# Causal attention with a channel mix: the reciprocals of the softmax sums go through TensorE as two fp16 parts instead of one fp32 operand, under a new plan

## The chip, the cores and the metric

The kernel runs on one core of one Trainium2 chip. The metric is the device time of one execution in microseconds, as the median of several runs. Three runs of the kernel before gave 539.42, 539.99 and 540.07 us.

## The reference

The inputs are `q`, `k`, `v` of shape (4, 12, 448, 64): 4 batches, 12 heads, 448 positions, head size 64, all fp32. Causal attention is followed by a channel mix with weights of 768 x 1024, 1024 x 768 and 768 x 768:

```python
scores = scale * np.matmul(q, k.transpose(0, 1, 3, 2))
scores = np.where(mask, -1000000000.0, scores)
scores = scores - np.max(scores, axis=-1, keepdims=True)
attn = np.exp(scores)
attn = attn / (np.sum(attn, axis=-1, keepdims=True) + 1e-09)
x = np.matmul(attn, v)          # heads side by side: (4, 448, 768)
x_prev = x moved down by one position
xk = mu_k * x + (1.0 - mu_k) * x_prev
xr = mu_r * x + (1.0 - mu_r) * x_prev
k = np.maximum(xk @ w_k, 0.0)
out = sigmoid(xr @ w_r) * (k * k @ w_v)
```

## The kernel before

The work is cut into 24 windows `w`, one for each pair of heads (6 pairs in each of 4 batches), and for each batch three rows of matmuls of the channel mix: `mk` (w_k), `mr` (w_r) and `mv` (w_v), all recorded at line 975.

A window goes through these steps. `score` (line 595) makes the scores of two heads, in fp32, as rows of 112 queries (4 chunks of 112), and adds the mask with small bf16 matmuls (line 616). `row_max` (line 630) takes the maxima on VectorE. `exps` (line 641) makes the exponentials on ScalarE, scaled up by 2^14, and adds up their sums into a tile `su` of 112 x 4 x 2: for each row of a chunk, 4 chunks and 2 heads. The exponentials stay undivided: `prob_hi` and `prob_lo` split them into two fp16 parts (lines 681 to 686), a transposing DMA turns them (line 692), and `weighted` (line 727) multiplies them with the values, 36 matmuls for a window (line 748); the first six windows are turned by TensorE in fp32 instead (`turn_e`, line 699), and take 24 matmuls at line 748.

The division is made at the end, on the transposed result, in which one position is one column. So the reciprocal of each sum has to stand in all 64 partitions of its head. That is done by four steps: `least` (line 658, ScalarE) adds the small constant to the sums, `recip` (line 661, VectorE) takes the reciprocals in place, `spread` (line 664, TensorE) multiplies a column of reciprocals, read as 64 equal columns, with the identity, so that row p of the chunk becomes column p in 64 partitions, and `spread_out` (line 678, VectorE or ScalarE) copies the result from PSUM to `xt`. `evac` (line 763) then multiplies the attention's result with `xt` and with a scale `xe` (line 938).

`spread` issues 8 fp32 matmuls for a window, 4 chunks by 2 heads. The two heads write to the lower and to the upper 64 partitions of one PSUM tile, from two column halves of TensorE. The profile shows each fp32 matmul as two records, 16 for a window. The tile has the tag `t`, whose pool has one buffer (line 386); the small steps that find one maximum over all partitions (`across`, line 448) and the idle matmuls share it.

The order of all instructions on all engines is made by a planner when the kernel is built (class `Plan`, line 35). Each step is entered by `plan.op` with its engine or engines, a cost in ns and the tiles that it reads and writes; steps that may run on one of several engines take ScalarE, VectorE or GpSimd as the plan has it, unless `by` in `CHOICE` (line 329) pins one. `l_load`, `l_att`, `l_wgh`, `l_mix`, `l_w` and `l_moe` in `CHOICE` lift a window's steps in the order, and `likes` favours engines. Every engine then works through its list in that order and waits, in order, for what an instruction needs. The planner fills long gaps of TensorE in the first 130 us with matmuls on a constant (`idle`, line 477). The four steps are entered in `weigh` (lines 1188 to 1199).

Of the kernel before, what the change touches and what calls it, by code (L numbers as in the profile page):

```python
# [11 lines left out]
F16 = mybir.dt.float16  # L12
# [3 lines left out]
AF = mybir.ActivationFunctionType  # L16
# [6 lines left out]
UP = 2.0**14  # L23
# [11 lines left out]
class Plan:  # L35
# [294 lines left out]
    "l_load": [-153, 304, 385, 144, 28, 153, 97, 60, -8, 105, 71, -20, 26, -303, 104, 894, -269, -9, -112, 27, 360, 271, -333, -282],  # L330
    "l_att": [-426, 60, 399, 122, 744, 836, 98, 213, 442, 308, 537, -143, -65, -254, 23, -108, -392, 2, 265, -623, 293, -35, -394, -101],
    "l_wgh": [201, -192, 134, 105, 94, 212, -70, -131, -5, 139, 268, 116, -88, 295, 32, -86, -103, -156, 1120, -19, 1254, 938, 84, 835],
    "l_mix": [4, 292, 190, 660, -23, -11, 615, -473, 183, 448, 126, -46, 601, 94, 297, 280, 72, 199, -539, -476, -538, -604, -1325, -922],
    "l_w": [568, 667, 632, -153, 139, 803, 1412, -163, 24, 385, 393, 544, 359, -208],
    "l_moe": [-11, -221, -117, 160, 236, -171, -183, -96, -366, 86, -327, -989],
    "chain": ["S", "S", "S", "S"],
    "ring": ["m", "m", "s", "s", "m", "m"],
    "pv": ["F", "F", "F", "F", "F", "F", "H", "H", "H", "H", "H", "H", "H", "H", "H", "H", "H", "H", "H", "H", "H", "H", "H", "H"],
    "likes": {"k_hi.DVE": 130, "w_lo.POOL": 0, "w_hi.ACT": -10750, "max_v.ACT": -70, "w_z.POOL": -100, "mix_lo.POOL": 270, "max_v.DVE": 430, "prob_hi.POOL": 800, "mix.DVE": 30, "r_copy.DVE": 30, "w_hi.DVE": -400, "parts_v.ACT": 30, "diff.POOL": 0, "w_hi.POOL": -1100, "mix.POOL": 0, "relu.DVE": 30, "prob_hi.ACT": 0, "r_copy.ACT": 180, "w_z.ACT": 0, "w_lo.DVE": 0, "whole.ACT": -1400, "w_z.DVE": 0, "mix_hi.ACT": -220, "relu.ACT": -1830, "k_hi.POOL": -160, "whole.DVE": 930, "diff.DVE": -100, "copy_e.DVE": 3060, "mix_hi.DVE": 210, "parts_v.POOL": 6050, "parts_v.DVE": 0, "mix_hi.POOL": 1170, "k_lo.POOL": -1000, "k_lo.DVE": -2100, "square.DVE": 370, "k_hi.ACT": -520, "mix_lo.DVE": 1300, "copy_e.ACT": -1000, "prob_lo.DVE": 1560, "prob_lo.POOL": -300, "spread_out.ACT": 1670, "spread_out.DVE": 570, "square.ACT": 0, "prob_hi.DVE": 1010},
# [6 lines left out]
def tile_causal_attention_channel_mix(  # L346
# [30 lines left out]

    const = ctx.enter_context(tc.tile_pool(name="const", bufs=1))
    wts = ctx.enter_context(tc.tile_pool(name="wts", bufs=1))
    act = ctx.enter_context(tc.tile_pool(name="act", bufs=1))  # L380
    p1 = ctx.enter_context(tc.tile_pool(name="p1", bufs=1))
    p2 = ctx.enter_context(tc.tile_pool(name="p2", bufs=2))
    ps_s = ctx.enter_context(tc.tile_pool(name="ps_s", bufs=NS, space=PSUM))
    ps_x = ctx.enter_context(tc.tile_pool(name="ps_x", bufs=1, space=PSUM))
    ps_m = ctx.enter_context(tc.tile_pool(name="ps_m", bufs=2, space=PSUM))
    ps_t = ctx.enter_context(tc.tile_pool(name="ps_t", bufs=1, space=PSUM))

    ident = const.tile([P, P], F32, name="ident")
    make_identity(nc, ident)
    busy = const.tile([P, P], F16, name="busy")  # L390
    nc.vector.memset(busy, 1.0)
    ones = const.tile([P, 1], F32, name="ones")
    nc.gpsimd.memset(ones, 1.0)

    pick = const.tile([P, 2, CP], BF16, name="pick")
    mask = const.tile([P, 2, CP], BF16, name="mask")
    for t, pattern, by, op, fill in (
        (pick, [[-D, 2], [1, CP]], -1, ALU.not_equal, 1.0),
        (mask, [[D, 2], [-1, CP]], 1, ALU.is_ge, masked),
    ):  # L400
        nc.gpsimd.memset(t[:D], 0.0)
# [174 lines left out]
    def parts_v(w, i, e):  # L576
        s = vsc[w // NPAIR][1][:CP]
        src = vraw[w]
        if i == 0:
            vs[w] = p2.tile([CP, 2, 2 * NCH, D], F16, tag="vs", name=f"vs_{w}", bufs=NVS)  # L580
            scaled(vs[w][:, 0], src, s, e)
        elif e == "D":
            nc.vector.scalar_tensor_tensor(
                vs[w][:, 1], src, s, vs[w][:, 0], ALU.mult, ALU.subtract
            )
        else:
            scaled(src, src, s, e)
            tt[e](vs[w][:, 1], src, vs[w][:, 0], ALU.subtract)

    vmm, em, stat, sps, tot, sm = {}, {}, {}, {}, {}, {}  # L590


    STEPS = [{0: 0, 1: CP}, {2: 0}, {3: 0}]

    def score(w, g):

        s = ps_s.tile([P, 2, 512], F32, tag="s", name=f"s_{w}_{g}")
        sps[w, g] = s
        for c, o in STEPS[g].items():
            n = CP * (c + 1)  # L600
            for j in range(2):
                rows = slice(64 * j, 64 * j + 64)
# [38 lines left out]
    def exps(w, g, j, c):  # L641
        if w not in tot:
            tot[w] = p2.tile([CP, NCH, 2], F32, tag="su", name=f"su_{w}")
        if (w, j) not in em:
# [6 lines left out]
            bias=stat[w][:, c, j : j + 1],  # L651
            scale=scale,
            accum_out=tot[w][:, c, j : j + 1],
        )

    def least(w):
        nc.scalar.activation(tot[w], tot[w], AF.Copy, bias=LEAST * UP)

    def recip(w):
        nc.vector.reciprocal(tot[w], tot[w])

    def spread(w):
        sm[w] = ps_t.tile([P, 512], F32, tag="t", name=f"sp_{w}")
        t = tot.pop(w)
        for c in range(NCH):
            for j in range(2):
                nc.tensor.matmul(  # L669
                    sm[w][64 * j : 64 * j + 64, c * CP : (c + 1) * CP],  # L670
                    t[:, c, j : j + 1].to_broadcast([CP, D]),
                    ident[:CP, :CP],
                    start=True,
                    stop=True,
                    skip_group_check=True,
                )
# [257 lines left out]
    def dm_scaled(r):  # L934
        g = const.tile([P, 3], F32, name="gprod")
        nc.vector.tensor_tensor(g[:, 0:1], r[:, 0:1], r[:, 1:2], ALU.mult)
        nc.vector.reciprocal(g[:, 1:2], g[:, 0:1])
        nc.vector.tensor_scalar(xe, wp[:, 0, :NPAIR], g[:, 1:2], 0.5, ALU.mult, ALU.mult)
        glob["mg"] = g[:, 0:1]
# [248 lines left out]
    def weigh(w):  # L1188
        if not whole_p(w):
            halve_v(w)  # L1190
        plan.lift = 1000 * CHOICE["l_wgh"][w]
        x = ("px", nexts("px"), 1)
        have["x"] = x
        tpt = [("pT", 2 * w + j, NPT) for j in range(2)]
        tu, t, xt = ("su", w, 2), ("t", nexts("t"), 1), ("x", w, 2)
        plan.op("ACT", 195, least, (w,), [(tu, None, "w")])
        plan.op("DVE", 205, recip, (w,), [(tu, None, "w")])
        plan.op("PE", 4 * 190 + 20, spread, (w,), [(tu, None, "r"), (t, None, "w")], rows=CP)
        plan.op(copied(S, True), 0, spread_out, (w,), [(t, None, "r"), (xt, None, "w")])
        for j in range(2):  # L1200
            te = ("e", 2 * w + j, NE)
            if whole_p(w):
                ring = CHOICE["ring"][w]
                for i, (a, z) in enumerate(PIECES):
                    t = (ring, nexts(ring), 2 if ring == "m" else NS)
                    inside = [c for c in range(NCH) if a <= first(c) < z]
                    plan.op("PE", (z - a) * 94 + 60, turn_e, (w, j, i), [(te, c, "r") for c in inside] + [(t, None, "w")], rows=CP)
                    plan.op(copied((z - a) * CP, True), 0, copy_e, (w, j, i), [(t, None, "r"), (tpt[j], i, "w")])
                continue
            at_ = nexts("p") - 1  # L1210
            tp = ("p", at_, 2)
            at_ = at_ % 2
            n = CP * NB
            plan.op(copied(n), 0, prob_hi, (w, j, at_), [(te, None, "r"), (tp, "h", "w")], fast=True)
            plan.op(less(n, True), 0, prob_lo, (w, j, at_), [(te, None, "r"), (tp, "h", "r"), (tp, "l", "w")], fast=True)
            plan.op("SP", 640, turn_p, (w, j, at_), [(tp, None, "r"), (tpt[j], None, "w")], dma=1960)
        if not whole_p(w):
            touch = [(t, None, "r") for t in tpt] + [(("vs", w, NVS), None, "r"), (x, None, "w")]
            plan.op("PE", sum(3 * (len(cs) * CP / 2.4 + 3) for _, cs in PV) + 20, weighted_all, (w,), touch, rows=CP)
        for n, (kb, cs) in enumerate(PV if whole_p(w) else []):  # L1220
            wide = len(cs) * CP / 2.4
            touch = [(t, i, "r") for t in tpt for i, (a, z) in enumerate(PIECES) if any(a <= first(c) < z for c in cs)]
            touch.append((("vraw", w, NPAIR), None, "r"))
            plan.op("PE", 4 * (wide + 3) + 20, weighted, (w, n), touch + [(x, None, "w")], rows=CP)
# [199 lines left out]
```

## Time and profile before

| what | us |
|---|---|
| median of 3 runs | 539.99 |
| the profiled execution, whole | 540.7 |
| its span, first to last instruction | 538.8 |
| TensorE busy | 511.9 (95%) |
| VectorE busy | 382.9 (71%) |
| ScalarE busy | 285.7 (53%) |
| GpSimd busy | 213.2 (40%) |

A share of busy time is an average over stages. The profile's names: PE is TensorE's matmuls, PEld its weight loads, DVE is VectorE, ACT ScalarE, POOL GpSimd and SP the engine that issues DMAs. `sp` is the PSUM tile of `spread`, `su` the sums, `x` the PSUM tile of the attention's result, `s` that of the scores. The granted clock (PEclk) is TensorE's clock as a share of 2.4 GHz; 0.5 is its other level, 1.2 GHz. The chain of waits is followed back from the last instruction, at each step to what released it.

### The profile page before, as it was taken

How to read it: one execution, taken by the hardware profiler on the slowest of the kernel's cores; microseconds unless marked ns; L12 is line 12 of the kernel's file. 1: busy time of each engine (PE TensorE's matmuls, PEld its weight loads, DVE VectorE, ACT ScalarE, POOL GpSimd, SP SyncE). 2: the span in 40 equal slices, each digit the busy share in tenths (PEclk: the TensorE clock that was granted, in tenths of full speed). 3: DMA queues.
4: the chain of work that ended last, by engine and by line, in shares of the span. 5: the costliest groups of instructions: out<-in, count | busy, mean ns of one | idle time of the engine just before them, and what ended most of it. 6: DMA issues, size and time to landing. Idle time of an engine off the chain costs nothing.

```text
span 538.8 us, 10303 instructions
## 1 busy us (share of the span) xinstructions
PE 511.9 (95%) x3905; PEld 290.7 (54%) x3905; DVE 382.9 (71%) x713; ACT 285.7 (53%) x742; POOL 213.2 (40%) x159
## 2 busy tenths in 40 slices
PE   8997799999999999999989999999999999999995
PEld 3454367664545555555546565654566556554552
DVE  1899999889976988868477768770798797307021
ACT  2687679766856586145437765352567750232400
POOL 4012234542643436753353475350697643003000
PEclk9998889999997999999999999999999999999998
DMA  8997127444744388567704678764248264300013
GB/s 226 331 296 240 39 84 189 119 149 139 132 71 90 69 150 155 106 112 117 143 18 95 125 134 151 142 113 75 41 91 128 54 123 85 68 2 0 1 34 69
DMA packets 207018, 60.71 MB, mean 113 GB/s; under 512 B 204396, under 2 KB 204408, under 8 KB 206200
## 3 DMA queue, kind: packets, MB, share of 16 engines
q1 hardware_dynamic: 206968, 60.05, 53.4%
q8 instruction: 31, 0.51, 0.4%
q14 instruction: 19, 0.16, 0.1%
HBM read 33.82 MB, written 5.51 MB: 73 GB/s over the span
## 4 chain that ended last, share of the span: by engine, by line
PE 83%; DVE 9%; ACT 3%; DMA 2%; issue 1%; SPq 1%; DVEq 0%; ACTq 0%
PE mk L975 20%; PE mv L975 20%; PE mr L975 14%; PE s L603 10%; PE x L748 7%; PE idle L480 4%; PE sp L669 4%; PE s L616 2%; DMA qraw<-in_q_dram 2%; DVE wz L897 1%; PE eT L706 1%; DVE wm L837 1%; DMA pT<-p 1%; DVE s L635 1%; DVE k L1045 1%
## 5 line engine op out<-in xcount | busy, mean ns | idle before, releaser
L647 ACT ACTIVATE e<-s,st 112x224 f32<-112x224 f32 (+1 forms) x192 | 92.9, 495 | 55.3 <-DVE st L638 43.3
L975 PE MATMUL mv<-k,wv 128*128 128x448 f16 x576 | 114.1, 353 | 0.0
L975 PE MATMUL mk<-xk,wk 128*128 128x448 f16 x576 | 111.7, 353 | 1.3 <-ACT a L987 1.3
L635 DVE TENSOR_REDUCE s<-s 112x2 f32<-112x224 f32 (+1 forms) x96 | 71.4, 744 | 29.0 <-PE s L616 23.3
L975 PE MATMUL mr<-xr,wr 128*128 128x448 f16 x432 | 88.6, 357 | 1.7 <-ACT a L1053 1.7
L975 PEld LDWEIGHTS <-wk 128*128 128x128 f16 x576 | 55.4, 98 | 53.4 <-issue 2.4
L975 PEld LDWEIGHTS <-wv 128*128 128x128 f16 x576 | 54.3, 98 | 50.3
L603 PE MATMUL s<-kT,qT 64*112 64x112 f32 (+3 forms) x384 | 63.7, 432 | 1.2 <-ACT e L647 1.0
L975 PEld LDWEIGHTS <-wr 128*128 128x128 f16 x432 | 40.8, 99 | 39.1 <-issue 3.7
L686 POOL TENSOR_TENSOR p<-e,p 112x1120 f16<-112x1120 f32 x20 | 48.9, 2453 | 31.0 <-ACT p L682 25.5
L480 PE MATMUL idle<-busy 128*128 128x512 f16 x178 | 45.0, 400 | 4.3 <-DVE wm L849 3.2
L987 ACT ACTIVATE a<-mk 128x448 f32<-128x448 f32 x26 | 14.1, 543 | 53.3 <-PE mk L975 53.3
L647 ACT ACTIVATION_READ_ACCUMULATOR e<-s,st 112x1 f32 x192 | 39.3, 205 | 0.0
L1064 DVE SCALAR_TENSOR_TENSOR a<-mv,kap,a 128x448 f32<-128x448 f32 x24 | 16.3, 677 | 31.9 <-PE mv L975 31.9
L603 PEld LDWEIGHTS s<-kT,qT 64*112 64x112 f32 x384 | 24.7, 174 | 19.9 <-issue 9.0
L686 DVE TENSOR_TENSOR p<-e,p 112x1120 f16<-112x1120 f32 x16 | 30.5, 1914 | 2.3 <-ACT p L682 2.2
L616 PEld LDWEIGHTS <-pick 64*112 64x112 bf16 x384 | 21.9, 128 | 18.4 <-issue 11.1
L799 POOL TENSOR_TENSOR xk<-xf,xk 128x448 f16<-128x448 f32 x16 | 18.6, 1160 | 32.4 <-ACT xk L795 24.0
L748 PE MATMUL x<-pT,vs 112*64 112x224 f16 (+1 forms) x648 | 30.6, 249 | 0.5 <-DMA pT<-p 0.5
L748 PEld LDWEIGHTS <-vs 112*64 112x64 f16 x648 | 28.0, 112 | 5.2 <-issue 3.7
L799 POOL TENSOR_TENSOR xr<-xf,xr 128x448 f16<-128x448 f32 x20 | 22.2, 1110 | 20.6 <-ACT xr L795 16.4
L480 PEld LDWEIGHTS <-busy 128*128 128x128 f16 x178 | 17.5, 102 | 23.5 <-issue 7.3
(162 smaller groups left out, 762.8 us busy)
## 6 DMA issues: line engine op xcount, KB each, us to landing
wraw<-in_moe_w_k_dram SPq DMA_DIRECT2D x6, 1024.0 KB, 6.7
wraw<-in_moe_w_v_dram SPq DMA_DIRECT2D x8, 768.0 KB, 4.7
vraw<-in_v_dram SPq DMA_DIRECT2D x24, 224.0 KB, 3.4
out_dram<-yT SPq DMA_DIRECT2D x48, 112.0 KB, 2.6
wraw<-in_moe_w_r_dram SPq DMA_DIRECT2D x6, 768.0 KB, 7.6
qraw<-in_q_dram SPq DMA_DIRECT2D x72, 56.0 KB, 2.2
kraw<-in_k_dram SPq DMA_DIRECT2D x72, 56.0 KB, 2.3
qraw<-in_q_dram SPq DMA_DIRECT2D x12, 112.0 KB, 6.5
```

The lines of the kernel that those rows point to most:

```text
L480: nc.tensor.matmul(t.rearrange("p (a b) -> p a b", a=4), busy, busy.unsqueeze(1).to_broadcast([P, 4, P]), start=True, stop=True,)
L603: nc.tensor.matmul(s[:CP, j, o : o + n], qkt[w, "q"][rows, c * CP : (c + 1) * CP], qkt[w, "k"][rows, :n], start=c == min(STEPS[g]), stop=F ...
L616: nc.tensor.matmul(s[:CP, j, o : o + CP], pick[rows, h, :], mask[rows, h, :], start=False, stop=h == 1, skip_group_check=True,)
L635: nc.vector.tensor_reduce(most[:, c - a, :], s[:CP, :, o : o + CP * (c + 1)], AX.X, ALU.max, negate=True)
L647: nc.scalar.activation(em[w, j][:, blocks(c)].rearrange("p a b -> p (a b)"), sps[w, g][:CP, j, o : o + CP * (c + 1)], AF.Exp, bias=stat[w] ...
L669: nc.tensor.matmul(sm[w][64 * j : 64 * j + 64, c * CP : (c + 1) * CP], t[:, c, j : j + 1].to_broadcast([CP, D]), ident[:CP, :CP], start=Tr ...
L686: tt[e](p[:, NB:, :CP], em.pop((w, j)), p[:, :NB, :CP], ALU.subtract)
L748: nc.tensor.matmul(px[w][64 * j : 64 * j + 64, cols], value(j, vi), p(j, pi), start=n == 0 and i == 0, stop=last and i == len(steps) - 1, ...
L799: tt[e](t[:, 1], xf.pop((w, mu)), t[:, 0], ALU.subtract)
L975: nc.tensor.matmul(ps, w[:, i, wi, cols], x[:, xi, t0 : t0 + n], start=(i == 0 and a == 0), stop=(i == steps - 1 and a == 2),)
L987: nc.scalar.activation(a, mps[m, "k", f][:, :n], AF.Relu)
L1064: nc.vector.scalar_tensor_tensor(s, mps.pop((m, "v", o))[:, : M[m][2]], kap[m][:, 3:4], s, ALU.mult, ALU.mult)
```

## The change

After `recip`, two new steps split the reciprocals: `recip_hi` casts them to fp16, and `recip_lo` subtracts the cast from them and writes the rest in fp16. Both may go to VectorE or GpSimd, `recip_hi` to ScalarE too. `spread` then multiplies both parts with an identity in fp16 and adds them up in PSUM: 16 fp16 matmuls for a window instead of 8 fp32. A constant `ident_h`, a cast of the identity on GpSimd, is new. `least` scales by 2^-28 as well, so that the reciprocals fit fp16, and `xe` takes this back with a changed constant. In the plan, `spread` has a cost of 4 * 97 + 20 ns in place of 4 * 190 + 20. All numbers of `CHOICE` but `chain`, `pv` and `turn` are changed, which gives a new order and other engines for many steps; `ring` of window 5 goes from "m" to "s".

```diff
 CHOICE = {
-    "l_wgh": [201, -192, 134, 105, 94, 212, -70, -131, ...],
+    "l_wgh": [256, -254, 127, 283, 90, 129, -132, -120, ...],
...
-    "ring": ["m", "m", "s", "s", "m", "m"],
+    "ring": ["m", "m", "s", "s", "m", "s"],
...
-    "likes": {"k_hi.DVE": 130, "w_lo.POOL": 0, ...},
+    "likes": {"k_hi.DVE": 160, ..., "recip_lo.POOL": -230, "recip_lo.DVE": 900, "recip_hi.DVE": -30, "recip_hi.ACT": 0, "recip_hi.POOL": 0},
-    "by": {"copy_e 0 1": "A", ...},
+    "by": {..., "recip_hi 0": "D", "recip_hi 1": "P", "recip_hi 13": "D", ..., "recip_lo 10": "D", "recip_lo 16": "P", "recip_lo 21": "P", "recip_lo 4": "P", ...},
...
     make_identity(nc, ident)
+    ident_h = const.tile([P, P], F16, name="identh")
+    nc.gpsimd.tensor_copy(ident_h, ident)
...
     def least(w):
-        nc.scalar.activation(tot[w], tot[w], AF.Copy, bias=LEAST * UP)
+        nc.scalar.activation(tot[w], tot[w], AF.Copy, bias=LEAST / UP, scale=UP**-2)
...
+    def recip_hi(w, e):
+        rs[w] = p2.tile([CP, 2, NCH, 2], F16, tag="rs", name=f"rs_{w}")
+        copy[e](rs[w][:, 0], tot[w])
+
+    def recip_lo(w, e):
+        tt[e](rs[w][:, 1], tot.pop(w), rs[w][:, 0], ALU.subtract)
+
     def spread(w):
         sm[w] = ps_t.tile([P, 512], F32, tag="t", name=f"sp_{w}")
-        t = tot.pop(w)
+        t = rs.pop(w)
         for c in range(NCH):
-            for j in range(2):
-                nc.tensor.matmul(
-                    sm[w][64 * j : 64 * j + 64, c * CP : (c + 1) * CP],
-                    t[:, c, j : j + 1].to_broadcast([CP, D]),
-                    ident[:CP, :CP],
-                    start=True,
-                    stop=True,
-                    skip_group_check=True,
-                )
+            for h in range(2):
+                for j in range(2):
+                    nc.tensor.matmul(
+                        sm[w][64 * j : 64 * j + 64, c * CP : (c + 1) * CP],
+                        t[:, h, c, j : j + 1].to_broadcast([CP, D]),
+                        ident_h[:CP, :CP],
+                        start=c == 0 and h == 0,
+                        stop=h == 1,
+                        skip_group_check=True,
+                    )
...
-        nc.vector.tensor_scalar(xe, wp[:, 0, :NPAIR], g[:, 1:2], 0.5, ALU.mult, ALU.mult)
+        nc.vector.tensor_scalar(xe, wp[:, 0, :NPAIR], g[:, 1:2], 0.5 * UP**-2, ALU.mult, ALU.mult)
...
-        plan.op("PE", 4 * 190 + 20, spread, (w,), [(tu, None, "r"), (t, None, "w")], rows=CP)
+        tr = ("rs", w, 2)
+        plan.op({"ACT": 195, "DVE": 160, "POOL": 240}, 0, recip_hi, (w,), [(tu, None, "r"), (tr, "h", "w")], fast=True)
+        plan.op({"DVE": 160, "POOL": 250}, 0, recip_lo, (w,), [(tu, None, "r"), (tr, "h", "r"), (tr, "l", "w")], fast=True)
+        plan.op("PE", 4 * 97 + 20, spread, (w,), [(tr, None, "r"), (t, None, "w")], rows=CP)
```

## Rows read from the trace of the kernel before

**Rows 1.** Busy time by stretch (us from the span's start): its length, then the busy time of PE, PEld, DVE, ACT and POOL with their instructions in brackets, the granted clock, the DMA share and GB/s.

```profile
0.00:70.00 70.00, 59.84 (x352) 32.11 (x353) 54.28 (x102) 41.89 (x89) 15.24 (x20) 0.93 0.76 218
70.00:115.00 45.00, 43.03 (x428) 28.89 (x427) 40.29 (x83) 36.43 (x111) 21.01 (x16) 0.99 0.52 136
115.00:532.00 417.00, 408.78 (x3130) 229.74 (x3127) 287.01 (x528) 207.37 (x545) 176.95 (x124) 0.99 0.51 93
532.00:539.00 7.00, 0.23 (x2) 0.00 (x0) 1.33 (x2) 0.00 (x0) 0.00 (x0) 0.71 0.35 66
```

**Rows 2.** The same stretches with the matmuls of line 669 (`spread`) alone: PE, PEld, clock, DMA.

```profile
0.00:70.00 70.00, 1.76 (x16) 1.41 (x16) 0.93 0.76 218
70.00:115.00 45.00, 4.88 (x80) 3.95 (x80) 0.99 0.52 136
115.00:532.00 417.00, 17.86 (x288) 14.00 (x288) 0.99 0.51 93
```

**Rows 3.** The same with the idle matmuls of line 480 alone.

```profile
0.00:70.00 70.00, 37.99 (x151) 15.10 (x151) 0.93 0.76 218
70.00:115.00 45.00, 7.01 (x27) 2.37 (x27) 0.99 0.52 136
115.00:532.00 417.00, 0.00 (x0) 0.00 (x0) 0.99 0.51 93
```

**Rows 4.** The page's shares of the chain that ended last, by engine.

```profile
PE 83%; DVE 9%; ACT 3%; DMA 2%; issue 1%; SPq 1%; DVEq 0%; ACTq 0%
```

**Rows 5.** The chain of waits in order of time: start, us, what. The five spreads of the first 115 us that stand on it.

```profile
67.75 1.71 PE sp L669 x16
...
81.77 0.92 PE sp L669 x16
...
87.18 0.92 PE sp L669 x16
...
98.15 0.99 PE sp L669 x16
...
112.78 0.77 PE sp L669 x16
```

**Rows 6.** The same chain, later pieces: a spread between the weighted sums and the channel mix, a spread behind a weighted sum, mask matmuls (L616), and the last row of matmuls.

```profile
266.42 0.20 PE s L616 x8
...
267.24 0.10 PE s L616 x4
...
282.88 0.92 PE sp L669 x16
283.79 1.45 PE x L748 x36
285.24 1.81 PE mr L975 x9
...
336.71 1.57 PE x L748 x36
338.28 0.80 PE sp L669 x16
...
524.86 7.39 PE mv L975 x39
```

**Rows 7.** Groups of small and of long instructions: line, engine, tile, shapes, count, busy us and mean ns of one, idle time before them.

```profile
L662 DVE RECIPROCAL su<-su 112x8 f32<-112x8 f32 x24 | 4.7, 194 | 2.0 <-ACT su L659 2.0
L659 ACT ACTIVATE su<-su 112x8 f32<-112x8 f32 x24 | 5.2, 219 | 0.1
L778 POOL TENSOR_TENSOR d<-xt 128x448 f32<-128x448 f32 x13 | 13.5, 1042 | 15.8 <-DVE xt L766 13.1 <-DVE wm L851 2.4
L686 POOL TENSOR_TENSOR p<-e,p 112x1120 f16<-112x1120 f32 x20 | 48.9, 2453 | 31.0 <-ACT p L682 25.5 <-DVE p L682 4.5 <-POOL p L686 0.7
L401 POOL MEMSET mask<- 64x224 bf16 x1 | 0.3, 279 | 0.0
L440 POOL TENSOR_TENSOR wr<-wz,ones 128x768 f16<-128x768 f32 x1 | 1.5, 1468 | 25.0 <-DVE wm L851 25.0
```

**Rows 8.** The timeline: a reciprocal and the spread that it releases, in the first 115 us (with the least time between them) and in the rest (again the least).

```profile
97.91 0.19 DVE L662 RECIPROCAL su<-su 112x8 f32<-112x8 f32 x1
98.15 0.99 PE L669 MATMUL sp<-ident,su 112*64 112x112 f32 x16 [0.23 <-DVE su L662]
...
402.12 0.19 DVE L662 RECIPROCAL su<-su 112x8 f32<-112x8 f32 x1
...
404.90 0.94 PE L669 MATMUL sp<-ident,su 112*64 112x112 f32 x16
```

**Rows 9.** The timeline of TensorE around 165 us and, for comparison, later: start, us, what, idle time before and its releaser.

```profile
159.52 0.73 PE L975 MATMUL mr<-xr,wr 128*128 128x448 f16 x3
161.27 0.38 PE L466 MATMUL bp_v<-dg_v,ones 1*128 1x1 f32 x2 [1.02 <-DVE dg_v L462]
162.31 1.22 PE L669 MATMUL sp<-ident,su 112*64 112x112 f32 x16 [0.66 <-DVE ac_v L472]
164.19 3.52 PE L975 MATMUL mr<-xr,wr 128*128 128x448 f16 x9 [0.67 <-ACT a L1053]
167.64 2.63 PE L748 MATMUL x<-pT,vs 112*64 112x224 f16 x36
...
176.36 1.64 PE L748 MATMUL x<-pT,vs 112*64 112x224 f16 x36
...
189.70 1.86 PE L975 MATMUL mv<-k,wv 128*128 128x448 f16 x9
```

More of the change, by code (lines that the diff above doesn't have):

```diff
@@ L329 @@
 CHOICE = {
[L330 to L333, printed above, removed]
@@ L334 @@
-    "l_w": [568, 667, 632, -153, 139, 803, 1412, -163, 24, 385, 393, 544, 359, -208],
-    "l_moe": [-11, -221, -117, 160, 236, -171, -183, -96, -366, 86, -327, -989],
+    "l_load": [-134, 274, 279, 104, 198, 87, 122, 133, -7, 150, 101, -61, -24, -271, 87, 891, -259, -61, -93, 3, 326, 307, -486, -311],
+    "l_att": [-378, -64, 231, 28, 723, 721, 35, 286, 455, 291, 586, -187, 68, -466, 27, -138, -493, 61, 308, -647, 128, -12, -465, -433],
+    "l_wgh": [256, -254, 127, 283, 90, 129, -132, -120, 7, 145, 254, 79, -97, 152, 230, 71, -225, -134, 1140, -41, 1228, 1066, 315, 948],
@@ L336 @@
+    "l_mix": [-3, 352, 240, 707, -43, -20, 500, -389, 183, 353, 138, -64, 702, 112, 240, 369, 219, 272, -511, -371, -329, -330, -1263, -1116],
+    "l_w": [574, 642, 589, -215, 171, 850, 1471, -24, 33, 651, 334, 466, 535, -331],
+    "l_moe": [-10, -212, -112, 123, 269, -217, -209, -118, -426, -60, -461, -1072],
     "chain": ["S", "S", "S", "S"],
-    "ring": ["m", "m", "s", "s", "m", "m"],
+    "ring": ["m", "m", "s", "s", "m", "s"],
     "pv": ["F", "F", "F", "F", "F", "F", "H", "H", "H", "H", "H", "H", "H", "H", "H", "H", "H", "H", "H", "H", "H", "H", "H", "H"],
-    "likes": {"k_hi.DVE": 130, "w_lo.POOL": 0, "w_hi.ACT": -10750, "max_v.ACT": -70, "w_z.POOL": -100, "mix_lo.POOL": 270, "max_v.DVE": 430, "prob_hi.POOL": 800, "mix.DVE": 30, "r_copy.DVE": 30, "w_hi.DVE": -400, "parts_v.ACT": 30, "diff.POOL": 0, "w_hi.POOL": -1100, "mix.POOL": 0, "relu.DVE": 30, "prob_hi.ACT": 0, "r_copy.ACT": 180, "w_z.ACT": 0, "w_lo.DVE": 0, "whole.ACT": -1400, "w_z.DVE": 0, "mix_hi.ACT": -220, "relu.ACT": -1830, "k_hi.POOL": -160, "whole.DVE": 930, "diff.DVE": -100, "copy_e.DVE": 3060, "mix_hi.DVE": 210, "parts_v.POOL": 6050, "parts_v.DVE": 0, "mix_hi.POOL": 1170, "k_lo.POOL": -1000, "k_lo.DVE": -2100, "square.DVE": 370, "k_hi.ACT": -520, "mix_lo.DVE": 1300, "copy_e.ACT": -1000, "prob_lo.DVE": 1560, "prob_lo.POOL": -300, "spread_out.ACT": 1670, "spread_out.DVE": 570, "square.ACT": 0, "prob_hi.DVE": 1010},
@@ new lines @@
+    "likes": {"k_hi.DVE": 160, "w_lo.POOL": 60, "w_hi.ACT": -8120, "max_v.ACT": -1000, "w_z.POOL": -100, "mix_lo.POOL": 0, "max_v.DVE": 0, "prob_hi.POOL": 430, "mix.DVE": 0, "r_copy.DVE": -970, "w_hi.DVE": -1000, "parts_v.ACT": 60, "diff.POOL": -100, "w_hi.POOL": 0, "mix.POOL": 100, "relu.DVE": 1140, "prob_hi.ACT": 100, "r_copy.ACT": -120, "w_z.ACT": 0, "w_lo.DVE": -240, "whole.ACT": -1340, "w_z.DVE": 0, "mix_hi.ACT": -250, "relu.ACT": -3830, "k_hi.POOL": 40, "whole.DVE": -100, "diff.DVE": -70, "copy_e.DVE": 0, "mix_hi.DVE": 210, "parts_v.POOL": 5620, "parts_v.DVE": 60, "mix_hi.POOL": 870, "k_lo.POOL": -400, "k_lo.DVE": -2640, "square.DVE": 370, "k_hi.ACT": 0, "mix_lo.DVE": 300, "copy_e.ACT": -630, "prob_lo.DVE": 590, "prob_lo.POOL": -300, "spread_out.ACT": 1670, "spread_out.DVE": 600, "square.ACT": 30, "prob_hi.DVE": 1010, "recip_lo.POOL": -230, "recip_lo.DVE": 900, "recip_hi.DVE": -30, "recip_hi.ACT": 0, "recip_hi.POOL": 0},
@@ L588, in parts_v @@
             tt[e](vs[w][:, 1], src, vs[w][:, 0], ALU.subtract)
-    vmm, em, stat, sps, tot, sm = {}, {}, {}, {}, {}, {}
+    vmm, em, stat, sps, tot, sm, rs = {}, {}, {}, {}, {}, {}, {}
     STEPS = [{0: 0, 1: CP}, {2: 0}, {3: 0}]
```

2 lines of the change are left out of this document (1 added, 1 removed).

## The prediction

> **What bounds the kernel now.** I first cut the span into stages by busy time [rows 1]. From 115 to 532 us, TensorE is busy for 408.8 of 417 us, with no idle matmul among them [rows 3], at a granted clock of 0.99; VectorE has 287 us there, ScalarE 207, GpSimd 177. This stage is TensorE's: what leaves its list moves the end, as long as no other wait takes its place. Of the 511.9 us that TensorE is busy in all, 45.0 are idle matmuls, all before 115 us [rows 3]. The first 70 us hold 38.0 of them and are not TensorE's. From 70 to 115 us TensorE is busy for 43.0 us, of which 7.0 are idle matmuls, so some 36 of 45 us are work: it often waits for the others. The last 7 us hold none of its work. The chain of waits agrees: 83% of it is TensorE [rows 4], five of the six spreads before 115 us are on it [rows 5], and later ones too [rows 6].
>
> Of the 24 spreads, 1 lies before 70 us, 5 between 70 and 115, and 18 after (16, 80 and 288 records, 16 for each) [rows 2].
>
> **One spread, before and after.** On the chain a spread takes 0.80 us behind a weighted sum, which uses the same column halves, and 0.92 behind other work; a weighted sum takes 1.45 behind a spread and 1.57 behind other work [rows 6]. So 0.12 us is the change of shape, which stays, and the work is 0.79.
>
> For the fp16 form I use two neighbours. A matmul of 448 columns takes 7.39/39 = 0.1895 us in the last row, so 112 columns are worth 0.047 [rows 6]. A window's weighted sum is 24 fp16 matmuls of 224 columns and 12 of 112, for two heads in the two column halves. If the halves run side by side, it is worth (12 x 224 + 6 x 112)/448 = 7.5 such matmuls, 1.42 us; it takes 1.45. So they do run side by side, and a pair of 112 columns takes about 0.049. The mask's small matmuls say the same: 8 take 0.20 and 4 take 0.10, 0.05 for a pair [rows 6]. The new spread has 8 pairs: 8 x 0.049 = 0.39 us. Saved: 0.79 - 0.39 = **0.40 us a spread**. Bounds: if each matmul took the weighted sum's mean (1.45/36 = 0.040), 16 would take 0.64 and 0.15 be saved; at 8 x 0.047 it is 0.41. I take 0.40, since the pieces of 112 columns are the nearest in shape.
>
> **Of these on the path.** In the stage from 115 us, 18 x 0.40 = **7.2 us**, all on the path. Before 115 us, five are on the chain, at most 5 x 0.40 = 2.0 us (the first, at 1.71 us, ran at the lower clock level and could give more). But there the two new steps can show: one spread starts 0.05 us after its reciprocal ends [rows 8]. Bounds 0 and 2.0; I take **1.0**.
>
> **What is added.** Each window gets two small elementwise steps on 8 columns. The nearest rows are the reciprocal on the same tile, 0.194 us on VectorE, and `least`, 0.219 on ScalarE; on GpSimd I have only a small fill of 0.279 and a subtraction of 448 columns of 1.042 as bounds [rows 7]. Both steps, with two handovers as short as the one above (0.05), take some 0.5 us, or up to 2.2 if both go to GpSimd at the upper bound. In the stage from 115 us the least time between a reciprocal and its spread is 404.90 - 402.31 = 2.6 us [rows 8]. That covers them: **0 us**. If the new order takes this cover away, each such window costs 0.5 us and more. As engine time, 48 x 0.2 = 9.6 us are spread over engines that are free for 130, 210 and 240 of 417 us [rows 1]: 0 as long as they fit between; queued behind the new steps are the copies and subtractions of the other windows, 0.2 us later each.
>
> The identity's cast is one instruction on GpSimd at the start, before GpSimd's wait of 25.0 us [rows 7]: 0; without that cover, a microsecond at the most by the row of 1.042. `least` and `xe` keep their instructions and change constants: 0. No DMA is added or moved past a queue by the fp16 form itself.
>
> **The new order.** It can't be read from the trace of before, and it moves steps, with their DMAs, on every queue, SP's and GpSimd's among them. I bound it by what the order can lose in one place. Around 162 us TensorE waits three times, 1.02 + 0.66 + 0.67 = 2.35 us, and then drops to the lower clock level: a spread of 1.22 us against 0.99, nine matmuls in 3.52 against 1.86, a weighted sum of 2.63 against 1.64, together 2.9 us lost [rows 9]. One such place costs 5.2 us. The new order may lose it (-5.2) or gain another (+5.2); without a row for either side I take 0.
>
> **Sum.** 7.2 + 1.0 = 8.2 us. The profiled execution took 540.7 us (span 538.8, and 1.9 around it): 540.7 - 8.2 = **532.5 us**. It lies 0.7 us above the median of the runs, 0.13%, less than this measurement can tell from no change (0.2%), so I leave it there.
>
> **Rivals.**
>
> *The weight loads set the pace.* The records of loads stay 16 for a spread [rows 2]: each fp32 matmul had two, and now 16 matmuls have one each. If each load, and not the columns, cost the 0.049 us that a record has now, 16 would take 0.79 as before and nothing be saved: 540.7 us. Against it: the weighted sum passes 36 loads of the same 64 columns in 1.45 us, 0.040 each [rows 6], and its length fits the columns. The Trainium skill, "TensorE: Matmul & The Clock Gate", section "LDWEIGHTS (loading the stationary operand)", puts a load at its columns divided by 1.2 ns, and "TensorEngine Tiling (Array Packing)", section "Restrictions", says that column tiling rules out the fast weight load. By that, 64 columns are an estimated 53 ns, and 16 in a row 0.85 us: no gain at all. By that rule the 36 loads would take 1.9 us, which the trace does not bear out, unless the two halves load side by side; then 8 x 53 ns = 0.43 us remain and the sum would be 0.7 us smaller. Chance 0.05.
>
> *One more stall of TensorE.* The new order puts one more place like that at 162 us into the long stage: 532.5 + 5.2 = 537.7 us. For it: 130 us of free VectorE time are not much when every step has a partner; against it: the planner now has 9.6 us less of TensorE's work to cover. Chance 0.16.
>
> *One stall fewer.* The place at 162 us goes: 527.3 us. Chance 0.10.
>
> *Slower: the spread waits for its low part.* TensorE takes its list in order, so a spread whose `recip_lo` is late holds up all behind it. `recip_lo` can stand on GpSimd behind a subtraction of 2.45 us [rows 7], or on VectorE behind a maximum. A wait of 2.45 us on TensorE is as long as the one at 162 us and can end with the lower clock level, so it costs up to 5.2 us. The saving of 8.2 us is gone from two such stalls on: 532.5 + 10.4 = 542.9 us. It decides where less than some 3 us lie between `recip` and the spread and GpSimd has a long step in front. Against it: of the 18 spreads in the long stage none has less than 2.6 us now [rows 8]. Chance 0.11.
>
> **How the numbers follow.** Forecast 0.58; with one stall more 0.16, with one fewer 0.10; load-bound 0.05; slower 0.11. Faster by over 0.2%: 0.58 + 0.16 + 0.10 = 0.84. Within 0.2%: 0.05. Slower: 0.11. The range takes in one stall fewer and, on the other side, one stall more and the load-bound case: 527.0 to 540.7. Left out are the slower case and a little below 527, some 0.14. The bounds of the unknown costs (0.15 for 0.40 us a spread: 4.5 us less gain; 0 or 2.0 before 115 us) lie within.
>
> **What would show it.** Right: the spread on the chain at some 0.40 us behind a weighted sum and 0.52 elsewhere, 16 records of 112 columns in fp16; TensorE's busy time after 115 us down by 7 us with its idle time there still near 8; the last row of matmuls beginning some 8 us earlier. Wrong in the price: a spread of 0.65 or more. Wrong in the cover: spreads, or weight loads of spreads, that wait for the new tile `rs`, and a granted clock under 0.99 behind them. Wrong about the order: idle time between 115 us and the end clearly above or below 8 us, or idle matmuls that now reach well past 115 us.

## The result and the profile after

The changed kernel took 547.13 us (median of 4 runs, 543.78 to 547.49) beside 540.03 for the kernel before: a ratio of 1.0116 with a 95% interval of 1.0074 to 1.0159. It is slower by some 6 us, where a gain of 7.5 us was forecast. Below, a difference in us is the measured ratio less 1, times 540 us, since every ratio was taken against runs of the kernel before. One execution of e1 took 1757.86 us, its other four 542.70 to 546.50, and e1's ratio leaves it out.

The spread itself became what was forecast. Groups of the kernel before, then of the changed one (line, engine, tiles, shapes, count, busy us and mean ns of one, idle before):

```profile
L669 PE MATMUL sp<-ident,su 112*64 112x112 f32 x384 | 24.5, 272 | 1.2 <-DVE ac_v L472 0.9 <-DVE su L662 0.2
...
L975 PE MATMUL mk<-xk,wk 128*128 128x448 f16 x576 | 111.7, 353 | 1.3 <-ACT a L987 1.3
```

```profile
L680 PE MATMUL sp<-identh,rs 112*64 112x112 f16 x384 | 14.7, 222 | 0.7 <-DVE xt L690 0.7
...
L986 PE MATMUL mk<-xk,wk 128*128 128x448 f16 x576 | 119.0, 365 | 1.2 <-DVE km L1016 1.2
```

The spreads fell from 24.5 to 14.7 us, 9.8 us in all, 0.41 a spread, and they waited 0.7 us in the whole run, none of it for the new tile. On the chain they take what [rows 6] led to, 0.52 us in place of 0.92:

```profile
193.01 0.51 PE sp L680 x16
...
197.61 0.52 PE sp L680 x16
```

What was gained was lost elsewhere, and the stretches show where (columns as in [rows 1], of the changed kernel):

```profile
0.00:70.00 70.00, 59.78 (x376) 31.90 (x376) 49.49 (x83) 45.53 (x102) 17.50 (x23) 0.98 0.78 224
70.00:115.00 45.00, 38.79 (x367) 25.75 (x368) 41.94 (x99) 34.17 (x98) 19.26 (x20) 0.89 0.43 113
115.00:190.00 75.00, 63.03 (x414) 32.90 (x414) 61.95 (x129) 42.65 (x119) 27.52 (x21) 0.86 0.46 96
190.00:539.00 349.00, 347.64 (x2759) 193.34 (x2753) 228.26 (x402) 166.43 (x436) 176.87 (x141) 1.00 0.54 92
```

Of the kernel before, the last two:

```profile
115.00:190.00 75.00, 72.54 (x536) 40.36 (x534) 64.08 (x137) 48.83 (x137) 30.87 (x21) 0.95 0.51 109
190.00:539.00 349.00, 336.48 (x2596) 189.38 (x2593) 224.25 (x394) 158.54 (x409) 146.08 (x104) 0.99 0.50 89
```

From 190 to 539 us TensorE of the changed kernel is without work for 1.4 us only. Before, it was 5.8 us from 190 to 532, where its work ended [rows 1]. But from 115 to 190 us it lacks work for 12.0 of 75 us, against 2.5, at a granted clock of 0.86 against 0.95, and from 70 to 115 the clock is 0.89 against 0.99. Over the span:

```profile
core 0: 538.8 us, clock 0.981
```

```profile
core 0: 545.7 us, clock 0.967
```

The first line is before, the second after. The account of the 6.9 us between the spans: the spreads -9.8; TensorE without any record 538.8 - 511.9 = 26.9 before and 545.7 - 509.4 = 36.3 after, +9.4; all its other records (487.4 and 494.7 us), +7.3. The `mk` matmuls alone grew by as much (111.7 to 119.0), the other groups evening out. Of this, 7.0 us are the 144 matmuls of the first batch, which run before 190 us, in the stretches with the low clock: 28.1 us before, 35.1 after. The idle matmuls stayed at 45 us.

The waits of TensorE of over 0.7 us between 124 and 170 us, in its timeline:

```profile
130.71 1.84 PE L605 MATMUL s<-kT,qT 64*112 64x448 f32 x4 [2.48 <-ACT e L649]
138.28 1.46 PE L605 MATMUL s<-kT,qT 64*112 64x112 f32 x8 [3.65 <-ACT e L649]
143.22 1.47 PE L605 MATMUL s<-kT,qT 64*112 64x336 f32 x4 [0.74 <-ACT e L649]
165.75 0.37 PE L457 MATMUL tp_gv<-ident,gvm 128*1 128x128 f32 x1 [4.04 <-DVE gvm L960]
```

Three scores wait for exponentials that have not yet emptied their PSUM tile, and a small transpose waits 4.04 us for VectorE's scales of w_v. Every channel-mix matmul behind them in the list waits too. None is in the chain of steps that the change edits: they are places of the new order. In e9 below, which has this order without the added steps, the same four instructions wait 2.07, 3.62, 0.97 and 4.05 us.

### The profile page after: what moved, and what is told of

It reads as the page before. It is cut to its first block, busy times and chain, and to the rows that moved or that the text cites. A ratio compares the mean times of both kernels' runs of the same rounds, so it can differ in the third digit from the quotient of the medians.

```text
span 545.7 us, 10395 instructions
## 1 busy us (share of the span) xinstructions
PE 509.4 (93%) x3908; PEld 283.9 (52%) x3908; DVE 383.0 (70%) x712; ACT 288.8 (53%) x754; POOL 241.1 (44%) x203
## 4 chain that ended last, share of the span: by engine, by line
PE 74%; DVE 13%; DMA 6%; issue 2%; ACT 2%; POOL 2%; SPq 0%; DVEq 0%; POOLq 0%; ACTq 0%
PE mv L986 21%; PE mk L986 15%; PE mr L986 14%; PE s L605 8%; PE x L759 7%; PE idle L482 4%; DMA pT<-p 2%; DVE s L637 2%; DVE wz L908 2%; DMA wraw<-in_moe_w_v_dram 2%; PE sp L680 2%; DMA mask<-mask 2%; PE s L618 1%; DVE wm L848 1%; DVE wz L906 1%
## 5 line engine op out<-in xcount | busy, mean ns | idle before, releaser
L649 ACT ACTIVATE e<-s,st 112x224 f32<-112x224 f32 (+2 forms) x192 | 92.7, 494 | 54.3 <-DVE st L640 46.5
L986 PE MATMUL mk<-xk,wk 128*128 128x448 f16 x576 | 119.0, 365 | 1.2 <-DVE km L1016 1.2
L986 PE MATMUL mr<-xr,wr 128*128 128x448 f16 x432 | 86.9, 353 | 0.1
L986 PEld LDWEIGHTS <-wk 128*128 128x128 f16 x576 | 56.7, 101 | 55.7 <-issue 8.3
L605 PE MATMUL s<-kT,qT 64*112 64x112 f32 (+3 forms) x384 | 67.3, 451 | 8.1 <-ACT e L649 7.8
L697 POOL TENSOR_TENSOR p<-e,p 112x1120 f16<-112x1120 f32 x24 | 58.5, 2442 | 21.9 <-ACT p L693 20.5
L986 PEld LDWEIGHTS <-wr 128*128 128x128 f16 x432 | 40.3, 98 | 36.3 <-issue 0.4
L998 ACT ACTIVATE a<-mk 128x448 f32<-128x448 f32 x27 | 14.7, 543 | 50.9 <-PE mk L986 46.6
L693 ACT CAST p<-e 112x1120 f16<-112x1120 f32 x25 | 28.0, 1128 | 22.3 <-DMA pT<-p 22.3
L797 DVE SCALAR_TENSOR_TENSOR xf<-d,muT,xt 128x448 f32<-128x448 f32 x38 | 31.2, 829 | 3.1 <-POOL xr L810 2.3
L759 PEld LDWEIGHTS <-vs 112*64 112x64 f16 x648 | 26.8, 110 | 6.3 <-issue 4.4
L442 POOL TENSOR_TENSOR a<-a,tf 128x448 f32<-128x448 f32 x11 | 13.1, 1192 | 32.5 <-DVE k L438 31.1
```

The lines of the kernel that those rows point to most:

```text
L605: nc.tensor.matmul(s[:CP, j, o : o + n], qkt[w, "q"][rows, c * CP : (c + 1) * CP], qkt[w, "k"][rows, :n], start=c == min(STEPS[g]), stop=F ...
L649: nc.scalar.activation(em[w, j][:, blocks(c)].rearrange("p a b -> p (a b)"), sps[w, g][:CP, j, o : o + CP * (c + 1)], AF.Exp, bias=stat[w] ...
L693: copy[e](p_t[at_][:, :NB, :CP], em[w, j])
L697: tt[e](p[:, NB:, :CP], em.pop((w, j)), p[:, :NB, :CP], ALU.subtract)
L759: nc.tensor.matmul(px[w][64 * j : 64 * j + 64, cols], value(j, vi), p(j, pi), start=n == 0 and i == 0, stop=last and i == len(steps) - 1, ...
L797: nc.vector.scalar_tensor_tensor(f, dx[w], m, x, ALU.mult, ALU.add)
```

## The experiments

All ratios are to the kernel before, those of the experiments to runs on the same chip. "Without the steps" means: the reciprocal is written in fp16 and the second part is a constant tile of zeros, so the result has the first part alone, with the same 16 matmuls. e9 to e14 give the reciprocals' tile six buffers, e6 the pool's own number.

| run | order | spread | added steps | ratio (95% interval) | us against 540 |
|---|---|---|---|---|---|
| the change | new | fp16 | new plan's | 1.0116 (1.0074 to 1.0159) | +6.3 |
| e1 | old | fp16 | VectorE | 1.0102 (1.0070 to 1.0135) | +5.5 |
| e1b | old | fp16 | VectorE | 1.0101 (1.0025 to 1.0177) | +5.5 |
| e2 | new | fp32 | none | 1.0274 (1.0235 to 1.0313) | +14.8 |
| e5 | old | fp32 | VectorE | 1.0102 (1.0072 to 1.0132) | +5.5 |
| e6 | old | fp16 | none | 0.9857 (0.9787 to 0.9927) | -7.7 |
| e7 | old | fp32 to window 5, then fp16 | VectorE from window 6 | 0.9998 (0.9967 to 1.0028) | -0.1 |
| e8 | old | fp16 | ScalarE, GpSimd | 0.9986 (0.9966 to 1.0007) | -0.8 |
| e9 | new | fp16 | none | 1.0122 (1.0091 to 1.0153) | +6.6 |
| e10 | old to k_scale, then new | fp16 | none | 0.9922 (0.9892 to 0.9952) | -4.2 |
| e14 | old to evac 5, then new | fp16 | none | 1.0063 (1.0033 to 1.0093) | +3.4 |
| e11 | new to k_scale, then old | fp16 | none | 1.0325 (1.0288 to 1.0362) | +17.6 |
| e12 | old, new first loads | fp16 | none | 0.9865 (0.9816 to 0.9915) | -7.3 |
| e13 | new, one step later | fp16 | none | 1.0026 (1.0003 to 1.0049) | +1.4 |
| e17 | old to k_scale, then new | fp32 to window 6, then fp16 | new plan's from window 7 | 0.9956 (0.9933 to 0.9978) | -2.4 |

e3 and e4 are e10 and e11 with both parts, with the steps on VectorE in the old order's share: 1.0060 (1.0038 to 1.0082) and 1.0365 (1.0336 to 1.0394).

**The form and the order, each alone (e1, e2).** e1 is the kernel before, its order untouched, with the new `spread` and this:

```diff
     def recip(w):
         nc.vector.reciprocal(tot[w], tot[w])
+        rs[w] = p2.tile([CP, 2, NCH, 2], F16, tag="rs", name=f"rs_{w}")
+        nc.vector.tensor_copy(rs[w][:, 0], tot[w])
+        nc.vector.tensor_tensor(rs[w][:, 1], tot.pop(w), rs[w][:, 0], ALU.subtract)
```

> The order, engines and idle matmuls of the kernel before, with the fp16 spread alone: both parts are made on VectorE right behind each reciprocal. Theory A (the fp16 form saves what was forecast and the new order loses it): 0.52 us a spread, TensorE's work down by some 9 us, waits and clock as before, so about 540 - 8 = 532 us, ratio 0.985. Rival B (the form itself costs: the two added steps make the spreads late or crowd VectorE): 540 us or more.

e2 is the changed kernel with the old `spread`; `recip_hi` and `recip_lo` do nothing:

> The new order with the fp32 spread of before; the two new steps issue nothing, and the sums' tile gets five buffers instead of two, since in the new order it would be freed too late otherwise. Theory A: the order is slow by itself, 547 + 8 = 555 us, ratio 1.028. Rival B (the form costs): near 540 us, ratio 1.00.

e2 came out as theory A had it, 554.5 us: the new order costs 14.8 us by itself, with the fp32 spread. e1 did not: 546.4 us. So the form as put into the old order costs too, and theory A was not the whole.

**Heads and rests, first try (e3, e4).** The order written out as a list, one kernel's up to a step and the other's for the rest: in e3 the old order ahead of the first `k_scale` and then the new one, in e4 the other way round:

```diff
     def run(self):
-        for i in self.order():
+        for x in ORDER.split():
...
```

> fp16 spread. Everything that the order of before issues ahead of the first batch's k_scale (about 154 us in its trace) in that order, with both parts on VectorE; the rest in the new order and on its engines. Theory A (all the loss lies in the first stretch, up to some 178 us of the new trace): the waits of the old head (some 15 us without work) and of the new rest (1.4 us), span about 526 us, time about 528 us, ratio 0.977, better than the old order throughout. Rival C (the rest of the new order loses too, or fits only its own head): 535 us or more.

> fp16 spread. Everything that the new order issues ahead of the first batch's k_scale (about 178 us in its trace) in that order; the rest in the order of before. Theory A: the loss of the new head stays, and the rest is a little worse than the new rest: 548 to 552 us, ratio 1.015 to 1.022. Rival C: 540 us or less.

Measured 543.1 and 559.9 us, 15 us above theory A's 528 and 8 above its 552. Both carry the steps on VectorE in the part in the old order. Those steps are what sets e1 apart from the forecast, so e3 and e4 settled nothing and were done again without them (e10, e11).

**The added steps (e1b, e5, e6, e7).** e1 ran again as e1b, for its trace, beside three others. e5 adds the two steps to the kernel before and uses nothing of them; e6 has the fp16 spread without them; e7 leaves windows 0 to 5 as before.

```diff
 e5, in recip:
+        nc.vector.tensor_copy(r[:, 0], tot[w])
+        nc.vector.tensor_tensor(r[:, 1], tot[w], r[:, 0], ALU.subtract)
 e6, in recip and spread:
-        nc.vector.reciprocal(tot[w], tot[w])
+        nc.vector.reciprocal(rs[w], tot.pop(w))
...
-                        t[:, c, j : j + 1].to_broadcast([CP, D]),
+                        (none_h if h else t)[:, c, j : j + 1].to_broadcast([CP, D]),
 e7, in recip (and the fp32 loop in spread):
+        if w < NPAIR:
+            return
```

> The same kernel as the first experiment (old order, fp16 spread, both parts on VectorE behind each reciprocal), for a profile at TensorE's normal clock and beside the next three. Again 543 to 547 us. Theory S (the added small steps on VectorE cost): single steps of 8 columns take 2 us instead of 0.17 where GpSimd runs a long step. Theory K (less matmul work before 115 us lets the clock fall): granted clock under the 0.93 and 0.99 that the stretches to 70 and from 70 to 115 us had before.

> The kernel before, with its fp32 spread, and the two small steps added on VectorE behind each reciprocal; what they write is not used. Theory S: slower by the steps' waits, 545 us or more. Theory K: the steps cost nothing, 540 us.

> Old order, 16 fp16 matmuls a spread, without the two steps: the reciprocal itself is written in fp16, and the second part is a constant tile of zeros, so the result has the first part alone. Theory S: the whole saving, about 532 us, ratio 0.985. Theory K: as slow as with the steps, 543 us or more.

> Old order; the first six windows (all spreads before 115 us) keep the fp32 spread and have no added steps, the other 18 go in fp16 with both steps on VectorE. Theory K: the head is as before and 18 x 0.40 = 7.2 us are saved, 533 us. Theory S with the steps of the head alone at fault: 533 too; with the later steps at fault: 540 or more.

Theory S holds: the steps alone cost 5.5 us (e5), and without them the fp16 spread saves 7.7 us (e6, interval 3.9 to 11.5), close to the forecast 8.2. With both, the steps cost 5.5 + 7.7 = 13 us (e1b against e6, uncertain by some 6). Theory K does not: e6 has as little matmul work as e1b, and its granted clock is 0.95 to 70 us and 1.00 from 70 to 115, where e1b has 0.92 and 0.85. e7, at 0 where 7.2 us were to be saved, says that the later steps cost too, not those of the head alone. e5's groups on VectorE:

```profile
L664 DVE CAST rs<-su 112x8 f16<-112x8 f32 x24 | 13.2, 552 | 0.8
L665 DVE TENSOR_TENSOR rs<-su,rs 112x8 f16<-112x8 f32 x24 | 10.6, 443 | 0.8
```

They take 23.8 us and not 48 x 0.17 = 8.2, which is what the undisturbed ones take. Its timeline at 418 us (VectorE and GpSimd) shows what they wait for:

```profile
417.71 2.31 POOL L689 TENSOR_TENSOR p<-e,p 112x1120 f16<-112x1120 f32 x1 [1.97 <-ACT p L685]
417.77 0.20 DVE L662 RECIPROCAL su<-su 112x8 f32<-112x8 f32 x1
418.01 2.04 DVE L664 CAST rs<-su 112x8 f16<-112x8 f32 x1
419.98 0.93 POOL L440 TENSOR_TENSOR a<-a,tf 128x448 f32<-128x448 f32 x1
420.08 0.85 DVE L665 TENSOR_TENSOR rs<-su,rs 112x8 f16<-112x8 f32 x1
```

The cast ends with GpSimd's subtraction (420.05 and 420.02), and the small subtraction ends with GpSimd's next step (420.93 and 420.91). The reciprocal, on the same tile and in the same GpSimd step, takes its 0.20 us. Of the 48 steps, 18 are stretched, to 0.6 us and more; each of them begins within a GpSimd step and ends 0.02 to 0.03 us behind one. The other 30 take 0.17.

**The steps on other engines (e8).**

```diff
-        nc.vector.tensor_copy(rs[w][:, 0], tot[w])
-        nc.vector.tensor_tensor(rs[w][:, 1], tot.pop(w), rs[w][:, 0], ALU.subtract)
+        nc.scalar.copy(rs[w][:, 0], tot[w])
+        nc.gpsimd.tensor_tensor(rs[w][:, 1], tot.pop(w), rs[w][:, 0], ALU.subtract)
```

> Old order, fp16 spread with both parts: the first on ScalarE, the second on GpSimd, right behind each reciprocal. Theory S (only VectorE's waits for GpSimd's steps were dear): 533 to 536 us, ratio 0.985 to 0.99, faster than the kernel before. Rival T (any step added to a full order costs some 6 us, wherever it runs): 540 us or more.

540.0 us, between the two: 6.3 us better than e1's placing, 6.9 worse than no steps (uncertain by 2 and by 4). The list of who waited for whom (engine, line, what it waited for: us in total, times, longest) names one reason:

```profile
POOL rs L667 <- ACT rs L666: 38.4, 10, 9.9
```

GpSimd stands for 38.4 us in all, in ten waits, until ScalarE has made the first part, and what is behind in its list stands too. How much of the 6.9 us this makes was not measured by itself.

**Where the new order loses (e9, e10, e11, then e12, e13, e14).** Without the steps, the same cuts again, and e9 with the new order throughout:

> The new order throughout, 16 fp16 matmuls a spread, without the two steps: the reciprocal is written in fp16, the second part is a constant tile of zeros, so the result has the first part alone. If the steps cost little where the new order puts them (two thirds on GpSimd and ScalarE): 545 to 547 us, as the changed kernel. If they cost what they do on VectorE in the old order (12 us): 535 us.

> fp16 spread without the two steps (first part alone). What the order of before issues ahead of the first k_scale, in that order; then the new order. Theory H (the new order's whole loss lies ahead of k_scale): 526 to 530 us, as fast as the old order throughout without the steps (534) or faster. Rival R (the new rest loses too): 538 us or more.

> fp16 spread without the two steps (first part alone). What the new order issues ahead of the first k_scale, in that order; then the order of before. Theory H: 545 to 552 us. Rival R: 538 us or less.

e9 equals the changed kernel (+6.6 and +6.3): **where the new plan puts the steps, they cost nothing that can be told** (within some 3 us). Only 8 of the 48 stand on VectorE there. So the change is -7.7 (the form, e6) and +14.3 (the order, e9 less e6; e2 had 14.8). By the intervals, a difference between two of these runs is uncertain by some 2 us, and one with e6 by some 4. e10 gives back 10.8 of the 14.3 by the old head alone. Its time missed the expected 526 to 530 but bears out that most of the loss lies ahead of `k_scale`. e11 was slower than expected, +17.6: behind the new head the old rest is 11 us worse than the new one. So what a rest costs depends on its head. e10's 3.5 us above e6 may be the price of such a seam, or of the new rest, or noise.

e14 moves the cut to the evac of window 5. e12 takes over only the new order's first loads, e13 moves one step of the new order (loads and steps written in short):

```diff
 e12, SP's first loads:
-  v0 v1 w0 q0 v2 w1 k0 v3 w2 q1 ...
+  v0 q0 v1 k0 w0 v2 q1 w1 v3 w2 ...
 e13, TensorE's list around 162 us:
-  turn(gv)  mk(6,1) mk(6,2) mk(6,3) mk(6,4) mk(6,5) mk(7,0)
+  mk(6,1) mk(6,2) mk(6,3) mk(6,4) mk(6,5) mk(7,0)  turn(gv)
```

> Old order, fp16 spread without the two steps (first part alone), and one thing of the new order: SP issues the loads of the first windows' q and k ahead of the first weight row, as the new order does. In the new order's trace the maximum of the first weight row starts 5.7 us later than before. Theory L (this is a large part of the loss): 538 to 540 us against 534 without. Rival (taken up by waits later on): 534 to 535.

> The new order, fp16 without the two steps, with one step moved: the small transpose of the w_v scales' maximum, for which TensorE waits 4.05 us in the new order, stands 6 channel-mix steps (18 matmuls, some 3.4 us) later in TensorE's list. If this wait and the lower clock behind it are lost time: 540 to 543 us against 546. If VectorE is late for all that follows anyway: 545 to 547.

> fp16 without the two steps. The order of before up to the evac of window 5 (about 119 us in its trace), then the new order. If the loss lies ahead of this point (loads, attention of the first batch): 534 to 537 us, as with the cut at k_scale (535). If it lies between the evac and k_scale: 543 to 547 us.

e12 is a null result: -7.3, as e6. The loads alone hardly made the first weight row's maximum late in that order (it starts at 12.8 us, against 12.1 before and 17.8 in the changed kernel), so it does not price the late start of the new order. e14 does, from above: +3.4, so 3.2 us lie ahead of that evac (e9 less e14) and 7.6 between it and `k_scale` (e14 less e10). TensorE's waits in e14 there are the four of the changed kernel and one more:

```profile
126.32 1.44 PE L700 MATMUL s<-kT,qT 64*112 64x336 f32 x4 [2.06 <-ACT e L744]
129.73 1.84 PE L700 MATMUL s<-kT,qT 64*112 64x448 f32 x4 [1.78 <-ACT e L744]
136.76 1.46 PE L700 MATMUL s<-kT,qT 64*112 64x112 f32 x8 [3.03 <-ACT e L744]
141.69 0.82 PE L700 MATMUL s<-kT,qT 64*112 64x336 f32 x4 [1.13 <-ACT e L744]
162.10 0.37 PE L552 MATMUL tp_gv<-ident,gvm 128*1 128x128 f32 x1 [4.05 <-DVE gvm L1056]
```

They add up to 12.05 us. e13 takes most of one of them away by moving a single small step:

```profile
162.59 0.27 PE L552 MATMUL tp_gv<-ident,gvm 128*1 128x128 f32 x1 [0.65 <-DVE gvm L1056]
```

It gets 5.2 us back (+6.6 to +1.4, uncertain by 2): as much as a stall with its lower clock was priced at from [rows 9]. The scores' waits were not moved, since the maxima behind them stand in VectorE's list; what they cost by themselves stays open.

**A version with both parts that is faster (e17).** Old order up to `k_scale` with the fp32 spread for windows 0 to 6, then the new order with its steps:

```diff
     def recip_hi(w, e):
+        if w < 7:
+            return
```

> The whole computation. What the order of before issues ahead of the first k_scale, in that order; windows 0 to 6 with the fp32 spread and without added steps; then the new order, in which windows 7 to 23 go in fp16 with both steps on the engines of the new plan. From 535 us without steps: + 7 x 0.40 for the fp32 spreads, + some 0.7 for the steps where the new plan puts them: 536 to 539 us, faster than before (540) by 0.3 to 0.7%. If the steps cost in the new rest as in the old order: 541 us or more.

537.94 us, 0.9956 (0.9933 to 0.9978): 2.4 us faster than the kernel before, the whole computation, and faster than the changed kernel.

## Why the prediction was wrong

*The price of a spread* was right: 0.40 us forecast, 0.41 measured, from 0.92 to 0.52 on the chain. The rival of the weight loads fell with it: 16 loads one after another would have left the spread at its 0.92 us.

*On the path* is borne out: 8.2 us forecast, 7.7 measured in the old order with the added steps left out (e6, interval 3.9 to 11.5 us).

*The added steps, 0 us*, rested on the wrong neighbour. I took the reciprocal's 0.194 us, since it has the same tile. The trace of before held steps of as few columns that were not cheap, and I did not read them:

```profile
L862 DVE TENSOR_TENSOR wp<-wp 128x6 f32<-128x6 f32 (+1 forms) x6 | 5.0, 837 | 0.2
...
L1027 DVE TENSOR_SCALAR tf<-cf,kap 128x8 f32<-128x8 f32 x4 | 4.5, 1126 | 0.1
```

Groups of 6 and 8 columns at 0.84 and 1.13 us say that a step's length is not its columns' there. In the old order the term is 5.5 to 13 us instead of 0. In the changed kernel, with 40 of the 48 steps off VectorE, it is 0 after all as far as can be told (e9); so this step failed as reasoning, but did not decide the result.

*The new order, 0 with bounds of 5.2 us*, is the step that failed. It was bounded by one place where the old order loses time; the new order has several such places between 120 and 166 us, and its price is 14.3 us. Of these, 3.2 lie ahead of the evac of window 5, 7.6 between it and `k_scale`, where those places are, and 3.5 behind it or at the seam. Only one place was priced by itself: the transpose, 5.2 us (e13). How the rest divides stays open. The bound should have come from the whole stretch in which orders can differ: the first 165 us, where TensorE of the kernel before already went without work for 14.6 us, did 45 us of idle matmuls and had a clock down to 0.93 [rows 1, 3]. There it is the other engines' results that decide, and TensorE's list that asked for one of them 4 us early lost 5.2 us by it.

*The slower rival* had the right side by the wrong mechanism. No spread waited for its low part (0.7 us of waits in all, for another tile). What stalled TensorE twice and more were scores and a transpose that the new order had put ahead of their inputs. GpSimd's subtraction of 2.45 us, which the rival feared ahead of `recip_lo`, did its harm ahead of the scales of w_v (last section). The point "two such stalls" and 542.9 us were too small as well.

*The marks that were to show it* did, for the order: TensorE's idle time from 115 us to the end of its work rose by 5 us to 13.3 (12.0 in 115 to 190 and 1.4 after), and 11 idle matmuls now stand behind 115 us. A clock under 0.99 had been named as a mark of spreads that wait for `rs`; it came from 70 to 190 us without such waits.

## What to carry to other kernels

When an edit comes with a new order, the edit and the order are two changes: run the edit in the old order and the old form in the new order before any of it is explained. Bound an order's price by the whole stretch in which engines depend on each other, not by one place of the old trace. And price a small step by the rows of steps with the same operands and the same neighbour on GpSimd, not by its number of columns.

## What the runs showed of the hardware

A VectorE step of 8 columns can take 2.2 us: in e5, the cast to fp16 and the subtraction of two SBUF tiles end when GpSimd's running step ends, while all 24 reciprocals keep their 0.18 to 0.20 us. The Trainium skill, "SBUF — State Buffer", section "Who interferes with whom", says that VectorE and GpSimd share one pair of ports as an exclusive lock for a whole instruction, taken by casts and copies in a two-port mode and by steps with two SBUF inputs. e5's trace agrees for both: 0.17 us alone, 2.04 and 0.85 us behind GpSimd steps of 2.31 and 0.93 us. Which mode the cast ran in, the trace does not say.

The scales of w_v, for which TensorE waited 4.04 us in the changed kernel, are such steps too (its timeline; VectorE and GpSimd):

```profile
159.58 2.45 POOL L697 TENSOR_TENSOR p<-e,p 112x1120 f16<-112x1120 f32 x1
159.79 2.27 DVE L871 TENSOR_SCALAR wp<-wm 128x8 f32<-128x8 f32 x1
161.99 1.03 POOL L810 TENSOR_TENSOR xr<-xf,xr 128x448 f16<-128x448 f32 x1
162.09 3.41 DVE L873 TENSOR_TENSOR wp<-wp 128x8 f32<-128x8 f32 x3
162.98 2.30 POOL L697 TENSOR_TENSOR p<-e,p 112x1120 f16<-112x1120 f32 x1
```

Four steps of 8 columns take from 159.79 to 165.50 us, beside three GpSimd steps, and the transpose behind them starts at 165.75. In the kernel before, the same four were held up for less time:

```profile
145.66 1.04 DVE L860 TENSOR_SCALAR wp<-wm 128x8 f32<-128x8 f32 x1
146.74 1.36 DVE L862 TENSOR_TENSOR wp<-wp 128x8 f32<-128x8 f32 x3
```

They took 2.40 us there and 5.68 here. So 3.3 of the 4.04 us that TensorE waits are, by an estimate that lets the four start when they did, time by which VectorE stood longer behind GpSimd: the new order put two of GpSimd's long subtractions beside them.
